# Attention and MLP backward pass on one core: the stores of the second to last pair move to GpSimd's queue in row pieces, and x is loaded in two pieces

## The chip, the core and the metric

The kernel runs on 1 core of a Trainium2 chip. The metric is the device time of one execution in microseconds (us). Sixteen DMA engines serve the core; a transfer is issued by one of the engine queues (SyncE, called SP; ScalarE, called ACT; GpSimd, called POOL), is cut into packets, and its packets are shared out over the DMA engines. Transfers issued by SP and ACT run on hardware rings, those issued by POOL on the software ring; in the profile these are the queues q1 (SP), q10 (ACT) and q0 (POOL). q8 and q14 carry instructions.

## What is computed

The forward function mixes a single-token attention block with a cache and a small MLP by a gate; the kernel returns its value and the gradients to nine inputs.

```python
q = (x @ wq).reshape(B, Sq, H, Dh)                  # Sq = 1, H = 32, Dh = 128, D = 640
scores = einsum("bhqd,bhkd->bhqk", q, k_cache) * Dh ** -0.5      # Sk = 4096
p = softmax(scores); o = einsum("bhqk,bhkd->bhqd", p, v_cache)
a = o.reshape(B, Sq, H * Dh) @ wo
h = B_x @ w1 + b1; b = (h * tanh(softplus(h))) @ w2              # F = 1728
g = sigmoid((x * gate_w).sum(-1))
out = g * a + (1 - g) * b                           # and the vjp with grad_out
```

Nearly all of the traffic is K and V, 32 MB each in bfloat16, which are read once, and dK and dV, of the same size, which are written once. dV of a head is the outer product of its softmax row and the gradient of its output, dK that of the score gradients and q.

## The kernel before

The 32 heads are worked in 16 pairs (`NP` = 16, numbered 0 to 15; `NP - 2` is pair 14). K or V of a pair is one tile `kv` of 128 partitions by 8192 bfloat16, 16 KB in each partition and 2 MB in all. Seven such buffers (`bufs`) are passed round: a load takes a buffer from `free_q`, VectorE writes the gradient over the loaded tile in place (`outer`, line 465, four quarters of 128x2048), the tile is stored, and the buffer goes back to `free_q`, where `pump` gives it to the next load. All loads of K and V are issued by SP. The order on every engine is written by hand: `slot(i, s)` lists what happens in each of 16 steps of pair i.

- Line 131 loads K or V; it waits until the store that frees the buffer has landed.
- `store_kv` (lines 734 to 738) issues the store of a pair's dV in step 13 of the pair and of its dK in step 3 of the next. While loads are left it is issued by POOL (25 stores); once the list of loads is empty it is issued by SP. Those are five: dK of pair 12, dV and dK of pair 13, dV and dK of pair 14.
- The last pair has no slots of its own after step 7. `last_dv(t)` and `last_dk(t)` make one quarter of dV or dK, and after quarters 1 and 3 SP stores the finished half (lines 875 and 881, 1 MB each).
- Between these quarters stand the sums and scalings for the gradients of `wq` (`dx_sum` on VectorE, `dwq_row` on ScalarE, stored by POOL, line 493) and of `wo` (`dwo_row` on ScalarE, stored by ACT, line 358), and behind them the final chain of small operations (lines 918 to 941) that ends in `frow`, three rows of 640 values which POOL stores (line 944).
- Lines 182 to 185 load x, gate_w, grad_out and b1 by POOL at the start; each is a tile of 128 partitions with a few values.

A store of 128 rows gives every DMA engine 8 rows of 16 KB: the 25 stores of POOL and the others of its kind show in the trace as 8 packets of 16,384 bytes on each of 16 engines.

Of the kernel before, what the change touches and what calls it, by code (L numbers as in the profile page):

```python
# [17 lines left out]
def kernel(  # L18
# [33 lines left out]
    nc = tc.nc  # L52
    P = 128
    _, H, Sk, Dh = A_k_cache.shape
# [3 lines left out]
    NP = H // 2  # L58
    NG = H // 8
    J = 64  # L60
# [26 lines left out]
    def vec_cols(v):  # L87
        return v.rearrange("(p c) -> p c", c=RC)

    x_v = A_x.rearrange("a b (p c) -> (a b p) c", c=RC)  # L90
    dy_v = grad_out.rearrange("a b (p c) -> (a b p) c", c=RC)
# [10 lines left out]
    def C(shape, dt, name):  # L102
        return const.tile(shape, dt, name=name, tag=name)
# [3 lines left out]
    bufs = [big.tile([P, bufw.get(i, KVW)], BF16, name=f"kv{i}", tag=f"kv{i}") for i in range(NBUF)]  # L107
# [4 lines left out]
    xc = C([P, RC], BF16, "xc")  # L112
    dyc = C([P, RC], BF16, "dyc")
    gwc = C([P, RC], BF16, "gwc")
# [7 lines left out]
    kbuf, vbuf, mbuf = {}, {}, {}  # L122
# [48 lines left out]
    def pump():  # L171
        while loads and (free_q or not loads[0][0]):
            loads.popleft()[1]()
# [5 lines left out]
        base=0, pattern=[[-1, P]], channel_multiplier=1,  # L179
    )  # L180
    pump()
    for t, src in ((xc[:], x_v), (gwc[:], vec_cols(gate_w)), (dyc[:], dy_v),
                   (b1c[:, 0:FK], B_b1[0:FM].rearrange("(p k) -> p k", k=FK)),
                   (b1c[0:FR, FK:FN], B_b1[FM:F].rearrange("(p o) -> p o", o=1))):
        nc.gpsimd.dma_start(t, src)
# [34 lines left out]
    def misc(shape, dt, name):  # L220
        return one_ps.tile(shape, dt, name=name, tag="misc")

    def chain(shape, dt, name):
        return one_ps.tile(shape, dt, name=name, tag="chain")
# [99 lines left out]
    def o_rows(g):  # L324
        ps = misc([P, 16, 8], F32, "o8_ps")
        nc.tensor.matmul(ps[:].rearrange("p a b -> p (a b)"), lhsT=od16[:].rearrange("p a b -> p (a b)"), rhs=idb[:],
                         start=True, stop=True)
        o8m = two.tile([P, 16, 8], F32, name="o8m", tag="o8m", bufs=1)
        nc.vector.tensor_tensor(o8m[:], ps[:], m16[:].unsqueeze(2).to_broadcast([P, 16, 8]), ALU.mult)
        nc.vector.reduce_sum(o8f[:], o8m[:].rearrange("p a b -> p b a"), axis=AX.X)  # L330
        nc.vector.tensor_copy(o8[:], o8f[:])

    def a_cols(g, c0=0, c1=RC):
        if c0 == 0:
            mst["a"] = misc([P, RC + W], F32, "a_ps")
        ps = mst["a"][:, 0:RC]
        wv = wob[g % 2][:].rearrange("p k (n c) -> p k c n", c=RC)
        for c in range(c0, c1):
            for k in range(8):
                nc.tensor.matmul(mst["a"][:, c:c + W], lhsT=wv[:, k, c, :], rhs=o8[:, k:k + 1].to_broadcast([P, W]),  # L340
                                 start=(k == 0), stop=(k == 7))
        if c1 == RC:
            if g == 0:
                nc.vector.tensor_copy(a_acc[:], ps)
            else:
                nc.vector.tensor_tensor(a_acc[:], a_acc[:], ps, ALU.add)

    def scaled(eng, dst, src, col):
        if eng is nc.vector:
            nc.vector.tensor_scalar(dst, src, col, None, ALU.mult)  # L350
        else:
            nc.scalar.mul(dst, src, col)  # L352
# [4 lines left out]
    def st_dwo(g, eng, k0=0, k1=8):  # L357
        eng.dma_start(dwo_v[g][:, k0:k1], wob[g % 2][:, k0:k1])
# [21 lines left out]
    def products(ps, src, c, col):  # L380
        for t in range(4):
            B = 4 * c + t
            for e in range(2):
                nc.tensor.matmul(ps[:, 4 * B:4 * B + W].rearrange("p (a b) -> p a b", b=4),  # L384
                                 lhsT=src[:, t, :, e],
                                 rhs=col[:, e, :, :].rearrange("p a b -> p (a b)").unsqueeze(1).to_broadcast([P, W // 4, 4]),
                                 start=(e == 0), stop=(e == 1))
# [74 lines left out]
    def outer(b, col, row, q):  # L462
        n = J // 4
        j0 = q * n
        nc.vector.tensor_tensor(  # L465
            kview(b)[:, j0:j0 + n, :].rearrange("p j (a b) -> p j a b", b=2),
            col[:, j0:j0 + n, :].unsqueeze(2).to_broadcast([P, n, Dh // 2, 2]),
            row.rearrange("p (a b) -> p a b", b=2).unsqueeze(1).to_broadcast([P, n, Dh // 2, 2]),
            ALU.mult)
# [5 lines left out]
    def dq_row(i):  # L475
        dqb = two.tile([P, 2], BF16, name="dqb", tag="dqb")
        nc.vector.tensor_copy(dqb[:], st[i]["dq"][:, 0:2])  # L477
        ps = chain([P, 2, P], BF16, "dqr_ps")
        for hh in range(2):
            nc.tensor.transpose(ps[:, hh, :], dqb[:, hh:hh + 1].to_broadcast([P, P]), idb[:])  # L480
        c = 256 * (i % 4)
        nc.scalar.copy(dqrow[(i // 4) % 2][:, c:c + 256].rearrange("p (a b) -> p a b", a=2), ps[:])
# [6 lines left out]
    def dwq_row(g, c0, c1, rc, eng=nc.scalar):  # L489
        scaled(eng, wqa[:, rc, g * GC + c0:g * GC + c1], dqrow[g % 2][:, c0:c1], xf[:, rc:rc + 1])  # L490

    def st_dwq(c0, c1, eng):
        eng.dma_start(dwq_v[:, :, c0:c1], wqa[:, :, c0:c1])
# [185 lines left out]
    for g in range(NG - 1):  # L679
        i = 4 * g + 4  # L680
# [16 lines left out]
    for g in (2, 3):  # L697
        i = 4 * g
# [8 lines left out]
    g, i = NG - 1, NP - 2  # L707
# [14 lines left out]
    def run_products(i, s):  # L722
# [5 lines left out]
        else:  # L728
# [2 lines left out]
                S_ps[n] = one_ps.tile([P, 2 * J + W], F32, name="S", tag="S")  # L731
            products(S_ps[n], src, s - 8, qR[(n // 4) % 2][:, n % 4])

    def store_kv(dct, i, dst, eng):
        b = dct[i]
        eng.dma_start(dst, bufs[b][:, 0:J * Dh])  # L736
        free_q.append(b)
        pump()

# [3 lines left out]
    def slot(i, s):  # L743
# [16 lines left out]
        if chain_on:  # L760
            if s == 0:
                dq_row(i - 1)
            if s in (0, 1, 3):
                dk_quarter(i - 1, (0, 1, 3).index(s) + 1)
            if s == 3:
                store_kv(kbuf, i - 1, dKv[i - 1], nc.gpsimd if loads else nc.sync)
            if s == 2:
                soft_max(i)
            if s == 4:
                soft_maxt(i)  # L770
            if s == 7:
                soft_z(i)
# [9 lines left out]
        if s in (9, 10, 12, 13):  # L782
            outer(vbuf[i], st[i]["p"], Dr[(i // 4) % 2][:, i % 4, :], (9, 10, 12, 13).index(s))
            if s == 13:
                store_kv(vbuf, i, dVv[i], nc.gpsimd if loads else nc.sync)
# [81 lines left out]
    i, g = NP - 1, NG - 1  # L867
# [3 lines left out]
    def last_dv(t):  # L871
        outer(vbuf[i], st[i]["p"], Dr[g % 2][:, q, :], t)
        if t % 2:
            h = slice((t - 1) * KVW // 4, (t + 1) * KVW // 4)
            nc.sync.dma_start(dVv[i][:, h], bufs[vbuf[i]][:, h])

    def last_dk(t):
        outer(fb, st[i]["ds"], Qr[g % 2][:, q, :], t)
        if t % 2:
            h = slice((t - 1) * KVW // 4, (t + 1) * KVW // 4)  # L880
            nc.sync.dma_start(dKv[i][:, h], bufs[fb][:, h])
# [12 lines left out]
    last_dv(0)  # L894
    for rc in range(RC):
        dwq_row(g, CA, CB, rc)
    o_rows(g)
    dq_row(i)
    last_dv(1)
    a_cols(g)  # L900
    for k in range(8):
        dwo_row(g, k)
        if k % 4 == 3:
            st_dwo(g, nc.scalar, k - 3, k + 1)
    last_dv(2)
    last_dv(3)
    last_dk(0)
    last_dk(1)
    for rc in range(RC):
        dx_sum(g, NG + g, CB, GC, rc)  # L910
        dwq_row(g, CB, GC, rc)
    st_dwq(g * GC + CA, (g + 1) * GC, nc.gpsimd)
    last_dk(2)
    last_dk(3)

    fin = C([P, 3, RC], BF16, "fin")
    ga = C([P, RC], F32, "ga")
# [8 lines left out]
                                   accum_out=dgp[:])  # L926
    dg_ps = chain([P, 1], F32, "dg_ps")
    nc.tensor.matmul(dg_ps[:], lhsT=ones_f[:], rhs=dgp[:], start=True, stop=True)
    dz = C([P, 1], F32, "dz")
    nc.vector.tensor_scalar(dz[:], dg_ps[:], g_all[:], omg[:], ALU.mult, ALU.mult)  # L930
    nc.vector.tensor_scalar(fin[:, 2, :], xf[:], dz[:], None, ALU.mult)
# [5 lines left out]
    fr_ps = misc([3, RC, P], BF16, "fr_ps")  # L937
    for c in range(RC):
        nc.tensor.transpose(fr_ps[:, c, :], fin[:, :, c], idb[:])
    frow = C([3, P, RC], BF16, "frow")  # L940
    nc.vector.tensor_copy(frow[:].rearrange("r p c -> r c p"), fr_ps[:])
    for r, v in enumerate((out_0.rearrange("a b n -> (a b) n"), out_1.rearrange("a b n -> (a b) n"),
# [31 lines left out]
```

## Time and profile before

| | us |
|---|---|
| three runs | 407.05, 407.87, 526.68 |
| median | 407.87 |
| the profiled execution, device time | 405.83 |
| its span, first to last instruction | 404.0 |

| engine | busy us | share of the span |
|---|---|---|
| TensorE matmul (PE) | 297.2 | 74% |
| VectorE (DVE) | 285.6 | 71% |
| ScalarE (ACT) | 246.8 | 61% |
| GpSimd (POOL) | 25.2 | 6% |

| DMA | |
|---|---|
| moved | 164.88 MB, mean 408 GB/s |
| read and written in HBM | 82.03 MB each |

The compute engines have idle time throughout; the DMA engines have hardly any before the last 12 us. The profile's lines name an engine, a line of the kernel, the operation, what is written and what is read. "SPq" and "POOLq" are the queues of SyncE and GpSimd, where DMAs are issued. The DMA share of a stretch of time is the mean over the 16 DMA engines, so that one engine alone is 1/16, or about 0.06.

### The profile page before, as it was taken

To read this page: it belongs to the slowest core of one execution; us is meant where nothing else is said; L and a number is where in the kernel's file an instruction comes from. 1 tells how busy PE (TensorE), PEld (TensorE's weight loads), DVE (VectorE), ACT (ScalarE), POOL (GpSimd) and SP (SyncE) were. 2 spreads that over 40 slices of the span, in tenths; PEclk is the share of its full clock that TensorE was granted. 3 is DMA by queue.
4 is the path that set the end of the run, shared out by engine and by line. 5 is a ranking of instruction groups with operands and counts; after the bars stand their busy time and mean duration, and the time that the engine had idled before them with its cause. 6 is when DMAs were issued, how large, how long until landed. Compare 5 with 4: busy or idle time off the path is not lost.

```text
span 404.0 us, 13041 instructions
## 1 busy us (share of the span) xinstructions
PE 297.2 (74%) x5654; PEld 272.9 (68%) x5657; DVE 285.6 (71%) x618; ACT 246.8 (61%) x507; POOL 25.2 (6%) x50
## 2 busy tenths in 40 slices
PE   4878996998885888673989869732989897987110
PEld 3558986877775777673889769732789786886100
DVE  2767695699975969583797839642695988597930
ACT  3555462586668678761766567731567996876800
POOL 3000100002000101000001000000000100000020
PEclk9999997998999899986999989985899998999555
DMA  8999999999999999999999999999999999999991
GB/s 275 426 399 434 420 423 417 430 418 420 423 422 427 391 421 429 427 431 430 428 423 428 426 427 426 425 426 432 431 406 400 414 428 419 422 430 422 420 386 44
DMA packets 15963, 164.88 MB, mean 408 GB/s; under 512 B 1713, under 2 KB 1905, under 8 KB 6178
## 3 DMA queue, kind: packets, MB, share of 16 engines
q1 hardware_dynamic: 8832, 94.08, 55.7%
q0 software_dynamic: 5472, 63.42, 37.3%
q10 hardware_dynamic: 1602, 6.56, 4.1%
q8 instruction: 44, 0.72, 0.7%
q14 instruction: 13, 0.11, 0.1%
HBM read 82.03 MB, written 82.03 MB: 406 GB/s over the span
## 4 chain that ended last, share of the span: by engine, by line
DMA 34%; issue 23%; PE 20%; DVE 12%; ACT 5%; POOL 2%; SPq 1%; POOLq 0%; ACTq 0%; DVEq 0%
DMA wq<-in_A_wq_dram 10%; DMA out_dram<-kv 8%; PE tr L374 8%; DVE kv L465 7%; DMA wq<-in_B_w_dram 6%; DMA wo<-in_A_wo_dram 5%; DMA kv<-in_A_k_cache_dram 5%; ACT tch L377 2%; PE dP L384 2%; PE o L433 2%; PE S L384 2%; PE dq L433 1%; PE q_ps L277 1%; PE a_ps L340 1%; DVE wq L486 1%
## 5 line engine op out<-in xcount | busy, mean ns | idle before, releaser
L374 PE MATMUL tr<-idf,kv 128*128 128x128 f32 x1024 | 172.1, 294 | 36.0 <-DMA kv<-in_A_v_cache_dram 20.0
L377 ACT COPY tch<-tr 128x512 f32<-128x512 f32 x256 | 144.2, 587 | 83.8 <-PE tr L374 78.6
L374 PEld LDWEIGHTS tr<-idf,kv 128*128 128x128 f32 x1024 | 118.6, 150 | 41.7 <-issue 36.9
L384 PEld LDWEIGHTS <-tch 128*128 128x128 bf16 x2048 | 89.5, 99 | 27.9 <-ACT tch L377 21.8
L465 DVE TENSOR_TENSOR kv<-p_dup,Dr 128x2048 bf16<-128x2048 bf16 x64 | 76.7, 1220 | 4.4 <-ACT p_dup L424 4.1
L465 DVE TENSOR_TENSOR kv<-ds_dup,Qr 128x2048 bf16<-128x2048 bf16 x64 | 76.8, 1220 | 0.4
L433 PEld LDWEIGHTS <-kv 128*128 128x128 bf16 x2048 | 59.1, 97 | 2.7 <-issue 1.6
L384 PE MATMUL dP<-dR,tch 128*128 128x48 bf16 x1024 | 47.3, 185 | 9.3 <-ACT tch L377 9.0
L384 PE MATMUL S<-qR,tch 128*128 128x48 bf16 x1024 | 48.1, 187 | 6.9 <-ACT tch L377 5.7
L290 DVE SCALAR_TENSOR_TENSOR junk<-wo,da_bc 128x640 bf16<-128x640 bf16 x32 | 26.3, 822 | 13.5 <-DMA wo<-in_A_wo_dram 12.7
L433 PE MATMUL o<-e_m,kv 128*128 128x48 bf16 x1024 | 32.4, 186 | 0.2 <-issue 0.2
L433 PE MATMUL dq<-ds_m,kv 128*128 128x48 bf16 x1024 | 30.6, 183 | 2.1 <-DVE ds_m L455 1.9
L736 POOL DMA_DIRECT2D out_dram<-kv x25 | 13.4, 537 | 296.0 <-DVE kv L465 278.6
L352 ACT ACTIVATE wq<-dqrow,xf 128x1024 bf16<-128x1024 bf16 (+2 forms) x30 | 25.1, 860 | 1.2 <-DVE wq L486 0.8
L486 DVE SCALAR_TENSOR_TENSOR wq<-wq,dqrow 128x1024 bf16<-128x1024 bf16 (+2 forms) x30 | 25.1, 863 | 0.2
L439 DVE TENSOR_TENSOR o<-o,rz 128x2 f32<-128x2 f32 x16 | 2.5, 158 | 26.5 <-PE o L433 26.5
L398 DVE TENSOR_REDUCE m<-S 64x1 f32<-64x64 f32 x32 | 7.0, 219 | 15.8 <-PE S L384 15.6
L424 ACT ACTIVATE p_dup<-e_m,rz 64x128 bf16<-64x128 bf16 x32 | 12.7, 397 | 7.8 <-DVE rz L418 7.4
L352 ACT ACTIVATE wo<-da_bc,o8f 128x640 bf16<-128x640 bf16 x20 | 15.9, 824 | 1.5 <-PE a_ps L340 0.9
L406 DVE TENSOR_REDUCE negM<-mt 64x1 f32<-64x64 f32 x32 | 7.1, 222 | 11.5 <-PE mt L403 10.8
L480 PE MATMUL dqr_ps<-idb,dqb 128*128 128x128 bf16 x32 | 4.9, 241 | 13.7 <-DVE dqb L477 13.7
L459 ACT COPY ds_dup<-ds_m 64x128 bf16<-64x128 bf16 x32 | 9.5, 297 | 8.1 <-DVE ds_m L455 7.6
(163 smaller groups left out, 253.2 us busy)
## 6 DMA issues: line engine op xcount, KB each, us to landing
out_dram<-kv POOLq DMA_DIRECT2D x25, 2048.0 KB, 19.8
kv<-in_A_v_cache_dram SPq DMA_DIRECT2D x16, 2048.0 KB, 19.8
kv<-in_A_k_cache_dram SPq DMA_DIRECT2D x15, 2048.0 KB, 20.6
out_dram<-kv SPq DMA_DIRECT2D x5, 2048.0 KB, 26.2
wo<-in_A_wo_dram SPq DMA_DIRECT2D x4, 1280.0 KB, 20.9
out_dram<-kv SPq DMA_DIRECT2D x4, 1024.0 KB, 20.5
out_dram<-wo POOLq DMA_DIRECT2D x3, 1280.0 KB, 26.8
wq<-in_A_wq_dram SPq DMA_DIRECT2D x2, 1280.0 KB, 9.5
```

What stands on the lines that cost most here:

```text
L290: nc.vector.scalar_tensor_tensor(junk[:], in0=wob[g % 2][:, k, :], scalar=1.0, in1=da_bc[:], op0=ALU.mult, op1=ALU.mult, accum_out=do8[g % ...
L352: nc.scalar.mul(dst, src, col)
L374: nc.tensor.transpose(tp[:, t, :], src[:, 4 * c + t, :], idf[:])
L377: nc.scalar.copy(dst[:].rearrange("p a b e -> p (a b e)").bitcast(F32), tp[:].rearrange("p a b -> p (a b)"))
L384: nc.tensor.matmul(ps[:, 4 * B:4 * B + W].rearrange("p (a b) -> p a b", b=4), lhsT=src[:, t, :, e], rhs=col[:, e, :, :].rearrange("p a b - ...
L406: nc.vector.tensor_reduce(negM[HS[hh]], mt[HS[hh], 64 * hh:64 * hh + 64], axis=AX.X, op=ALU.max, negate=True)
L424: nc.scalar.activation(p[HS[hh]], e_m[i % 2][HS[hh], :, hh].unsqueeze(2).to_broadcast([64, J, 2]), ACT.Copy, scale=st[i]["rz"][HS[hh], hh: ...
L433: nc.tensor.matmul(st[i][key][:].rearrange("p (a b) -> p a b", b=2), lhsT=src[:, j, :], rhs=rhs[:, j, :].unsqueeze(1).to_broadcast([P, W / ...
L459: nc.scalar.copy(ds[HS[hh]], ds_m[i % 2][HS[hh], :, hh].unsqueeze(2).to_broadcast([64, J, 2]))
L465: nc.vector.tensor_tensor(kview(b)[:, j0:j0 + n, :].rearrange("p j (a b) -> p j a b", b=2), col[:, j0:j0 + n, :].unsqueeze(2).to_broadcast ...
L486: nc.vector.scalar_tensor_tensor(w, in0=w, scalar=1.0, in1=dqrow[g % 2][:, c0:c1], op0=ALU.mult, op1=ALU.mult, accum_out=dq_acc[:, rc, par ...
L736: eng.dma_start(dst, bufs[b][:, 0:J * Dh])
```

## The change

Three things are edited. The store of dV of pair 14 becomes three transfers of 4, 120 and 4 rows and that of dK of pair 14 three of 13, 105 and 10 rows, all issued by POOL. The load of x becomes two transfers, of 60 and 68 rows. In the work of the last pair five of the quarters are moved: `last_dv(1)` ahead of `o_rows` and `dq_row`, `last_dv(2)` to where `last_dv(1)` was, `last_dk(1)` behind the `wq` sums, and `last_dk(2)` and `last_dk(3)` into the final chain, behind the two groups of matmuls in it.

```diff
-    for t, src in ((xc[:], x_v), (gwc[:], vec_cols(gate_w)), (dyc[:], dy_v),
+    for t, src in ((xc[0:60], x_v[0:60]), (xc[60:P], x_v[60:P]), (gwc[:], vec_cols(gate_w)), (dyc[:], dy_v),
...
+    late = {(True, NP - 2): (4, 120, 4), (False, NP - 2): (13, 105, 10)}
+
     def store_kv(dct, i, dst, eng):
         b = dct[i]
-        eng.dma_start(dst, bufs[b][:, 0:J * Dh])
+        p0 = 0
+        for n in late.get((dct is vbuf, i), (P,)):
+            (nc.gpsimd if n < P else eng).dma_start(dst[p0:p0 + n], bufs[b][p0:p0 + n, 0:J * Dh])
+            p0 += n
         free_q.append(b)
         pump()
...
     last_dv(0)
     for rc in range(RC):
         dwq_row(g, CA, CB, rc)
+    last_dv(1)
     o_rows(g)
     dq_row(i)
-    last_dv(1)
+    last_dv(2)
     a_cols(g)
     for k in range(8):
         dwo_row(g, k)
         if k % 4 == 3:
             st_dwo(g, nc.scalar, k - 3, k + 1)
-    last_dv(2)
     last_dv(3)
     last_dk(0)
-    last_dk(1)
     for rc in range(RC):
         dx_sum(g, NG + g, CB, GC, rc)
         dwq_row(g, CB, GC, rc)
     st_dwq(g * GC + CA, (g + 1) * GC, nc.gpsimd)
-    last_dk(2)
-    last_dk(3)
+    last_dk(1)
...
     nc.tensor.matmul(dg_ps[:], lhsT=ones_f[:], rhs=dgp[:], start=True, stop=True)
+    last_dk(2)
     dz = C([P, 1], F32, "dz")
...
         nc.tensor.transpose(fr_ps[:, c, :], fin[:, :, c], idb[:])
+    last_dk(3)
     frow = C([3, P, RC], BF16, "frow")
```

The bytes that are moved, and every compute instruction, are the same before and after; five DMA instructions are added (four on net for the stores, one for x), and two of SP's leave its queue for POOL's.

## The prediction

> **What bounds the kernel now.** I read the page first, its slices and its DMA queues.
>
> ```profile
> DMA  8999999999999999999999999999999999999991
> GB/s 275 426 399 434 420 423 417 430 418 420 423 422 427 391 421 429 427 431 430 428 423 428 426 427 426 425 426 432 431 406 400 414 428 419 422 430 422 420 386 44
> ...
> q1 hardware_dynamic: 8832, 94.08, 55.7%
> q0 software_dynamic: 5472, 63.42, 37.3%
> ```
>
> From the second slice to the second last the DMA engines are full, at about 425 GB/s, whatever the compute engines do. An edit to compute is therefore worth nothing unless it lets a DMA engine run dry. The queue lines give the price of a row: q0 moved 63.42 MB in 37.3% of 16 x 404.0 us, 2,411 us of engine time, so 16,384 bytes take 0.62 us on one DMA engine; q1 (94.08 MB, 55.7%) gives 0.63. The two rings cost the same per byte.
>
> The last slice is empty, so I then read the busy time of the last stretches.
>
> ```profile
> 390.00:392.00 2.00, 0.00 (x0) 0.00 (x0) 0.00 (x0) 0.00 (x0) 0.81 (x2) 0.50 0.99 407
> 392.00:394.00 2.00, 0.00 (x0) 0.00 (x0) 0.00 (x0) 0.00 (x0) 0.00 (x0) 0.50 0.59 243
> 394.00:396.00 2.00, 0.00 (x0) 0.00 (x0) 0.00 (x0) 0.00 (x0) 0.00 (x0) 0.50 0.29 118
> 396.00:398.00 2.00, 0.00 (x0) 0.00 (x0) 0.00 (x0) 0.00 (x0) 0.00 (x0) 0.50 0.07 29
> 398.00:400.00 2.00, 0.00 (x0) 0.00 (x0) 0.00 (x0) 0.00 (x0) 0.00 (x0) 0.50 0.06 25
> 400.00:402.00 2.00, 0.00 (x0) 0.00 (x0) 0.00 (x0) 0.00 (x0) 0.00 (x0) 0.50 0.07 29
> 402.00:404.00 2.00, 0.00 (x0) 0.00 (x0) 0.00 (x0) 0.00 (x0) 0.00 (x0) 0.50 0.00 0
> ```
>
> The last two columns are the DMA share and GB/s. From 392 to 396 the engines fall out one by one; from 396 to 402 the share is 0.06 to 0.07, which is 1/16: one DMA engine works alone for 6 us. In the packet records its last packets are 8192-byte packets of q1, end to end, the last done at 402.2; the other fifteen end between 391.7 and 396.1, at 394.1 in the mean. The waits of SP's queue say the same.
>
> ```profile
> SPq L969 <- DMA out_dram<-wq: 11.2, 1, 11.2
> SPq L969 <- DMA out_dram<-kv: 7.3, 1, 7.3
> ```
>
> After its last issue SP waits 11.2 us for the store of `wq`, then 7.3 us more for the last half of dK. The chain of waits ends in `frow` and shows none of this, so it isn't used. The lateness is old: of the last load of V fifteen shares landed between 355.7 and 360.1 and the sixteenth at 365.7. The records carry no engine number.
>
> **The change, part by part.** *Row pieces.* Both whole stores give each DMA engine 8 rows, so 16 together. If the piece of 120 is 8 rows on each of fifteen engines and that of 105 is 7 on each, and the same engine is left out of both, it keeps only its share of the small pieces: 0 to 4 rows, 12 to 16 fewer, or 7.5 to 10 us at 0.625. The 4 + 4 + 13 + 10 = 31 single rows go mostly to the others, which then have 15 + 2 = 17 rows against 16, +0.6 us (+1.2 for an engine with 18). No transfer of before shows an uneven split of wide rows, so I bound it: at best the late engine ends at 402.2 - 7.5 = 394.7 or sooner; at worst it is not the one left out and ends at 402.8. In the first case the other fifteen set the end, 396.1 + 0.6 = 396.7, a gain of 5.5 us. I take this one: a piece of 120 or 105 rows has a whole split over 15 and none over 16, so one engine is spared, and the edit names the same one for both.
>
> [...]
>
> *Issue.* POOL's stores take 0.53 us each, SP's 0.33. Six issues put 3.2 us on POOL, in order ahead of the `wq` store at 361.4, which moves to about 366. POOL waited 19.6 us before that store and 21.7 before the next; nobody reads these tiles again. SP loses two issues. Cost 0; if POOL were full, up to 3.2 us. POOL's issues also wait for the landing of its eighth issue before; for the last `frow` rows those are now the dV pieces of about 359, which have 28 us to land against a median of 26.2 for such stores on SP. Cost 0 to 1, off the path.
>
> *Order of rings.* 4 MB move from q1 to q0 at 358 and 365. V of pair 15 has mostly landed by 360, and no later load exists, so no compute waits longer. With both rings full an engine alternates; the total per engine is unchanged. Cost 0.
>
> *Quarters moved.*
>
> ```profile
> 377.33 2.36 DVE L465 TENSOR_TENSOR kv<-ds_dup,Qr 128x2048 bf16<-128x2048 bf16 x2
> ...
> 381.33 2.36 DVE L465 TENSOR_TENSOR kv<-ds_dup,Qr 128x2048 bf16<-128x2048 bf16 x2
> ...
> 387.07 1.91 DVE L941 COPY frow<-fr_ps 3x640 bf16<-3x640 bf16 x1 [0.79 <-PE fr_ps L939]
> 389.27 1.53 POOL L944 DMA_DIRECT2D out_dram<-frow  x3 [4.51 <-DVE frow L941]
> ```
>
> A quarter is 1.14 us (2.27 for two). dV's first half goes out some 1.5 us sooner (before at 374.2), dK's first half about 1 later (1.73 us of `wq` sums come ahead of its second quarter, less 0.8 gained above). Its second half waits also for the final chain: from dk1's end near 380.7, 0.85 of small operations, 1.14, 1.1, 1.14: issued near 385.0 instead of 383.7. `frow` fills its two waits for PE with these quarters and leaves near 387.2 instead of 389.3. At 385 the engines still have about 9 us of work, of which that half is 1 MB / 425 GB/s = 2.5 us, so 6.5 us lie ahead of it: cost 0. If an engine ran dry there, it would cost the 1.3 us of delay.
>
> *x.* One more POOL issue, 0.54 us, ahead of gate_w. VectorE waits 1.33 us for gate_w at 8.58, so the first stage starts about 0.5 us later. The prefetched loads and the stores of 41.3 and 47.2 keep the DMA engines full past 60 us, so the cover holds: 0, else 0.5.
>
> **Sum.** 402.2 to 396.7 is -5.5 us; all else 0 to +1.3. On the profiled execution, 405.83 - 5.5 = 400.3 (span 398.5). The two close runs are 1.2 and 2.0 us above that execution; the mean of the three is 406.9, so I expect 401.4 in unprofiled runs. Against the median of 407.87 that is -1.6%.
>
> **Rivals.**
> - *The late engine isn't the spared one.* Nothing in the records says which it is. It then gets up to one row more: 405.83 + 0.6 = 406.4, or 407.5 from the mean. For it: any of sixteen engines could be meant. Against it: the lateness is steady, 5 to 9 us in each of SP's transfers from 340 on, so it is one engine, which a fixed choice of rows can hit. [...]
> - *Slower: the pieces fall on few engines.* If 120 rows went to 8 engines and 105 to 7 (15 each), an engine in both would have 30 rows and some 2 single ones instead of 16: 16 x 0.625 = +10 us, so that the late one ends at 412.2, device time 415.8, 416.9 from the mean; on one engine the 105 rows alone are 65 us. It decides from 15 rows more on the late engine (9.1 us, from the mean to 2% above the median). For it: the only odd transfer of before, one row on ACT, has one data packet. Against: the 64-row transfers of `w2` land with their 128-row neighbours (25.4 and 25.8 us).
> - *Deeper gain.* If the single rows fall on the early ones of the fifteen and the order evens the rest, the end is their mean, 394.1, plus 0.6: a gain of 7.5, 399.4 from the mean, and a little over half of such cases below the 2% line.
>
> **Chances.** Forecast 0.60, at 401.4, its own range 398.8 to 404. Spared the wrong engine 0.18, near 407.5. Few engines 0.08, 416 and up. Deeper gain 0.14. A measurement of this kernel tells about 2%, 8.2 us, from no change, so faster means below 399.7. Faster: 0.08 of the deeper case and 0.10 of the forecast's low side = 0.18. Slower: 0.08. Same: 0.74. The range takes in the forecast, nearly all of the deeper gain, and the wrong engine: 398.3 to 408.3.
>
> **What would show it.** The lone engine's 6 us at the end must be gone: a DMA share that falls from 1.0 to 0 within some 5 us, with the last kv landing near 397 and SP's last wait for kv near 1 to 2 us instead of 7.3. The wrong engine shows as the same six microseconds at 0.06; few engines as a long stretch at 0.06 to 0.5 after 396. The second dK half should be issued near 385 and `frow` near 387, with a DMA share of 1.0 until 392; a dip there would break the claim that the moved quarters cost nothing. A GB/s below 415 between 360 and 385 would show that pieces cost more than whole stores, which I priced at nothing.

## The result, and the profile after

The changed kernel takes 416.86 us (median of 4 runs, 415.8 to 417.18) against 407.46 us for the kernel before (median of 4), a ratio of 1.0239, 95% interval 1.0201 to 1.0276: slower by 9.4 us (one run of the kernel before, the 526.68 us of the table, is far off and not in the ratio). The forecast was 401.4 and the range ended at 408.3, so the time is outside it. The profiled execution took 415.8 us, with a span of 414.0.

The page of the changed kernel, the slices and the two large DMA queues:

```profile
DMA  8999999999999999999999999999999999999980
GB/s 269 424 401 419 427 419 427 424 416 380 427 428 416 394 422 429 429 430 426 427 429 424 430 426 426 426 427 428 429 417 421 423 423 413 427 346 274 333 336 39
...
q1 hardware_dynamic: 8544, 89.89, 52.7%
q0 software_dynamic: 5904, 67.61, 40.0%
```

The DMA row reads 9 from the second slice to the third last, much as before: the engines count as busy. The row under it tells another story. A slice is 10.35 us here, and in slices 36 to 39, from 362 to 404 us, the engines move 346, 274, 333 and 336 GB/s; the same four slices of the kernel before had 430, 422, 420 and 386. From 370 to 380 us the share is 0.96 at 274 GB/s against 1.01 at 425 before: the share hides a loss of rate that the bytes show. The stretches of the end, of the changed kernel and then three of the kernel before (the last two columns are DMA share and GB/s, the one ahead of them the granted TensorE clock):

```profile
360.00:370.00 10.00, 8.14 (x175) 7.70 (x174) 8.60 (x24) 8.03 (x18) 3.98 (x7) 1.00 1.01 380
370.00:380.00 10.00, 3.57 (x92) 3.07 (x88) 3.93 (x10) 2.70 (x7) 0.00 (x0) 0.71 0.96 274
380.00:390.00 10.00, 2.58 (x44) 2.39 (x44) 8.91 (x26) 7.03 (x11) 0.00 (x0) 0.50 0.95 303
390.00:400.00 10.00, 0.69 (x5) 0.41 (x5) 3.80 (x7) 1.42 (x4) 2.36 (x4) 0.50 1.00 386
400.00:404.00 4.00, 0.00 (x0) 0.00 (x0) 0.00 (x0) 0.00 (x0) 0.00 (x0) 0.50 0.56 229
404.00:406.00 2.00, 0.00 (x0) 0.00 (x0) 0.00 (x0) 0.00 (x0) 0.00 (x0) 0.50 0.19 77
406.00:408.00 2.00, 0.00 (x0) 0.00 (x0) 0.00 (x0) 0.00 (x0) 0.00 (x0) 0.50 0.14 57
408.00:410.00 2.00, 0.00 (x0) 0.00 (x0) 0.00 (x0) 0.00 (x0) 0.00 (x0) 0.50 0.09 35
410.00:412.00 2.00, 0.00 (x0) 0.00 (x0) 0.00 (x0) 0.00 (x0) 0.00 (x0) 0.50 0.04 16
```

```profile
360.00:370.00 10.00, 7.88 (x171) 7.38 (x171) 7.77 (x27) 6.89 (x17) 0.84 (x1) 1.00 1.00 420
370.00:380.00 10.00, 3.70 (x107) 3.46 (x107) 8.54 (x16) 7.74 (x15) 0.00 (x0) 0.77 1.01 425
380.00:390.00 10.00, 1.25 (x7) 0.91 (x7) 7.28 (x24) 3.23 (x7) 1.55 (x3) 0.50 1.01 423
```

Two things are to be seen. The rate falls in the stretch in which POOL issues the first three pieces, at 360.09; and the thin tail, a share of 0.19 to 0.04 from some late engines and at last a single one, is still there, from 404 to 411. The kernel before moved 420, 425 and 423 GB/s in the three stretches from 360 to 390, so 0.40 + 1.51 + 1.20 = 3.1 MB were not moved there, which take 7.3 us at 425 GB/s, of the 10.0 us by which the span grew.

The two waits of SP's queue after its last issue:

```profile
SPq L974 <- DMA out_dram<-frow: 18.4, 2, 17.4
...
SPq L974 <- DMA out_dram<-kv: 0.5, 1, 0.5
```

The wait for `kv` has shrunk from 7.3 to 0.5, as the forecast asked. It proves nothing: SP now waits up to 17.4 us for the store of `frow` first, and the `kv` lands 0.5 us after that. How a long wait is shared out between two names says only which transfer the late engine finishes last: the last shares of `frow` and of the last `kv` land at 411.14 and 411.73.

The records of single packets give the size of it. All packets of 16 KB on the two rings between 362 and 390 us, mean and longest, in ns:

| kernel | mean | longest |
|---|---|---|
| before | 616 | 1006 |
| after | 831 | 2844 |
| before 360 us, both | 619 to 621 | |

### The profile page after: what moved, and what is told of

Same layout as the page of the kernel before. It is cut to its first block, busy times and chain, and to the rows that moved or that the text cites. A ratio compares the mean times of both kernels' runs of the same rounds, so it can differ in the third digit from the quotient of the medians.

```text
span 414.0 us, 13053 instructions
## 1 busy us (share of the span) xinstructions
PE 299.8 (72%) x5657; PEld 276.3 (67%) x5657; DVE 285.0 (69%) x618; ACT 247.2 (60%) x507; POOL 28.8 (7%) x57
## 4 chain that ended last, share of the span: by engine, by line
DMA 34%; issue 24%; PE 21%; DVE 10%; ACT 4%; POOL 2%; SPq 1%; DVEq 0%; POOLq 0%; ACTq 0%
DMA wq<-in_A_wq_dram 9%; PE tr L374 8%; DMA out_dram<-kv 7%; DMA kv<-in_A_k_cache_dram 6%; DMA wq<-in_B_w_dram 6%; DVE kv L465 6%; DMA wo<-in_A_wo_dram 5%; PE o L433 2%; PE dq L433 2%; PE dP L384 2%; ACT tch L377 2%; PE S L384 2%; PE q_ps L277 1%; PE a_ps L340 1%; POOL out_dram L740 1%
## 5 line engine op out<-in xcount | busy, mean ns | idle before, releaser
L433 PEld LDWEIGHTS <-kv 128*128 128x128 bf16 x2048 | 60.1, 98 | 8.7 <-issue 7.6
L740 POOL DMA_DIRECT2D out_dram<-kv x31 | 16.5, 533 | 314.8 <-DVE kv L465 292.4
L433 PE MATMUL dq<-ds_m,kv 128*128 128x48 bf16 x1024 | 31.5, 184 | 7.7 <-issue 5.3
L482 ACT COPY dqrow<-dqr_ps 128x256 bf16<-128x256 bf16 x16 | 6.1, 379 | 14.8 <-PE dqr_ps L480 14.8
```

The lines of the kernel that those rows point to most:

```text
L433: nc.tensor.matmul(st[i][key][:].rearrange("p (a b) -> p a b", b=2), lhsT=src[:, j, :], rhs=rhs[:, j, :].unsqueeze(1).to_broadcast([P, W / ...
L740: (nc.gpsimd if n < P else eng).dma_start(dst[p0:p0 + n], bufs[b][p0:p0 + n, 0:J * Dh])
```

## The experiments

The experiments of one group ran on one chip and share their runs of the kernel before.

### First group: which part, and is it the ring or the row pieces

Theory one after the result: a store of fewer than 128 rows runs at a lower rate than a whole one, whatever ring it is on. Rivals: the software ring is slower here, or delays the loads of V; or the moved quarters let the engines run dry.

**e1_whole_on_pool**: all of the change, but each of the two stores is one transfer of 128 rows, issued by POOL.

```diff
-    late = {(True, NP - 2): (4, 120, 4), (False, NP - 2): (13, 105, 10)}
+    late = {(True, NP - 2): (P,), (False, NP - 2): (P,)}
...
-            (nc.gpsimd if n < P else eng).dma_start(...)
+            (nc.gpsimd if (dct is vbuf, i) in late else eng).dma_start(...)
```

> The changed kernel with the two stores of pair 14 whole, 128 rows each, but still on POOL's ring; x in two pieces and the quarters moved as in the change. Theory A (the row pieces themselves slow the DMA packets: 16 KB packets take 0.61 us before 360 us and 0.86 to 0.99 us on average between 365 and 390 in the changed kernel): all packets back at 0.61 us, GB/s of 360 to 390 back above 410, ratio to before 0.995 to 1.005. Theory B (two more whole stores on the software ring late in the kernel cost the time, cut or not): ratio 1.015 to 1.025, packets slow as in the change. Theory C (the moved quarters and x starve the DMA engines): ratio 1.02.

Measured: 406.34 us (10 runs) against 406.21 (19), ratio 1.0014 (1.0002 to 1.0026). Its stretches:

```profile
360.00:370.00 10.00, 8.23 (x190) 7.81 (x186) 8.31 (x23) 8.03 (x18) 1.59 (x3) 1.00 1.01 424
370.00:380.00 10.00, 4.30 (x116) 3.83 (x112) 8.46 (x19) 6.06 (x12) 0.00 (x0) 0.78 1.00 422
380.00:390.00 10.00, 1.25 (x7) 0.91 (x7) 8.04 (x23) 5.09 (x9) 2.33 (x4) 0.50 1.01 424
```

The rate is whole again. So the ring, together with x and the quarters, costs 0.3% at most, and the loss hangs on the cut into rows.

**e2_pieces_alone**: the kernel before with the row pieces only (x whole, quarters where they were).

```diff
+    late = {(True, NP - 2): (4, 120, 4), (False, NP - 2): (13, 105, 10)}
```

> The kernel before with the row pieces (4, 120, 4; 13, 105, 10) on POOL alone; x whole, no quarter moved. Theory A: ratio 1.02 to 1.03, slow packets between 360 and 395 us. Theory C: ratio 0.985 to 1.00. [...]

Measured: 414.63 us (4 runs), ratio 1.0204 (1.0185 to 1.0223): 8.4 us of the 9.4.

```profile
360.00:370.00 10.00, 7.88 (x171) 7.38 (x171) 7.77 (x27) 6.85 (x18) 2.46 (x4) 1.00 1.03 368
370.00:380.00 10.00, 4.57 (x107) 4.16 (x107) 4.13 (x10) 3.79 (x10) 0.00 (x0) 0.65 0.93 274
380.00:390.00 10.00, 0.56 (x2) 0.50 (x2) 9.15 (x24) 7.23 (x12) 0.84 (x1) 0.50 0.98 326
```

The same low rates as in the changed kernel, without the other two edits.

**e3_x_and_quarters**: the change without the row pieces; both stores stay whole on SP's ring.

```diff
-    late = {(True, NP - 2): (4, 120, 4), (False, NP - 2): (13, 105, 10)}
+    late = {}
```

> The changed kernel with the stores of pair 14 left whole on SP as before: x in two pieces and moved quarters alone. Theory A and B: ratio 0.995 to 1.005, one DMA engine alone for some 6 us at the end as before. Theory C: ratio 1.02.

Measured: 407.05 us (10 runs), ratio 1.0026 (1.0011 to 1.0040). The two other edits cost something, about 1 us, and are no part of the large loss.

**e4_halves_64**: the kernel before with both stores cut evenly, 64 + 64 rows on POOL. Sixty-four rows divide evenly over sixteen engines, 4 rows each, so that no engine need be spared; in e5 such stores reach 16 packets of 16 KB under way. From e1 it differs in the number of rows of a transfer, and in that x and the quarters are as before.

```diff
+    late = {(True, NP - 2): (64, 64), (False, NP - 2): (64, 64)}
```

> The kernel before with both stores of pair 14 in two pieces of 64 rows on POOL. Each piece splits evenly, 4 rows on each of 16 engines, so no engine gets more than before. [...] Theory A2 (what costs is the uneven split over 15 or fewer engines): packets at 0.61 us, ratio 0.995 to 1.005.

Measured: 410.07 us (4 runs), ratio 1.0121 (1.0071 to 1.0172).

```profile
360.00:370.00 10.00, 8.13 (x185) 7.71 (x181) 8.31 (x24) 8.01 (x18) 2.62 (x5) 1.00 1.02 360
370.00:380.00 10.00, 5.09 (x115) 4.48 (x110) 5.38 (x14) 4.38 (x10) 0.00 (x0) 0.70 1.01 283
380.00:390.00 10.00, 0.56 (x2) 0.50 (x2) 9.12 (x26) 6.76 (x12) 0.83 (x1) 0.50 0.97 326
...
404.00:406.00 2.00, 0.00 (x0) 0.00 (x0) 0.00 (x0) 0.00 (x0) 0.00 (x0) 0.50 0.13 53
406.00:408.00 2.00, 0.00 (x0) 0.00 (x0) 0.00 (x0) 0.00 (x0) 0.00 (x0) 0.50 0.02 8
```

An even cut loses the rate as well: the missing bytes, 0.60 + 1.42 + 0.97 = 3.0 MB, are as many as with the uneven pieces. So it is not the uneven split. Yet the kernel is only 3.9 us late by the medians (4.9 by the ratio; one of its four runs took 414.16, as long as e2), and the tail of one engine is nearly gone (0.13 and 0.02 instead of six microseconds at 0.06 and more). Why the late engine catches up here and not in the changed kernel was not settled.

### The disputed cost by itself

**e5_stores_alone**: computes nothing of the reference. It loads one tile of V and stores it into the places of dV and dK in different ways, each way after the one before has landed (a write to the first column of the tile stands between); every other output stays unwritten. Where a way's last store does not read that column, the next way starts beside it: so the end of the column halves overlaps with the start of the HBM block, and the end of that with the four neighbouring rows on POOL, which are therefore read from SP's ring alone.

```diff
+    phase(g, whole, 2)
+    phase(g, pieces(64, 64), 2)
+    phase(g, pieces(4, 120, 4), 2)
+    phase(g, pieces(13, 105, 10), 2)
+    phase(g, cols, 2)         # 128 rows, two halves of the columns
+    phase(g, block, 2)        # half the columns of 128 rows into 64 whole rows of HBM
+    phase(g, four(0, 1), 1)   # 4 neighbouring rows; then every 4th, every 32nd
...
+    phase(s, whole, 2)        # the same on SP's ring
+    phase(s, pieces(64, 64), 2)
+    phase(s, pieces(4, 120, 4), 2)
```

> A kernel that computes nothing of the reference: one 2 MB tile of V is loaded, and then stored in one way after another, each way alone on the chip (the next waits until the last has landed), 4 MB each unless said otherwise. On POOL's ring: whole; 64 + 64 rows; 4 + 120 + 4; 13 + 105 + 10; 128 rows in two halves of the columns; 128 rows by half of the columns written to the 1 MB of HBM that 64 rows fill; then single stores of 4 rows of 16 KB taken from neighbouring partitions, from every fourth, and from every 32nd partition. Then on SP's ring: whole; 64 + 64; 4 + 120 + 4; the three of 4 rows. [...] Theory A2 (the uneven split costs): 64 + 64 as fast as whole. Theory A3 (the rows of a piece collide in HBM): the half-column stores into the 64-row region are as slow as 64 + 64. Theory B2 (a matter of the software ring): slow on POOL, fast on SP.

Its stretches, one for each way; a row has busy time of VectorE and POOL, the granted clock, DMA share and GB/s. In order: whole, 64 + 64, 4 + 120 + 4, 13 + 105 + 10, column halves and the HBM block on POOL; whole, 64 + 64 and 4 + 120 + 4 on SP.

```profile
10.00:20.00 10.00, 0.00 (x0) 0.00 (x0) 1.00 0.97 408
22.00:40.00 18.00, 0.00 (x0) 0.96 (x2) 1.00 0.92 226
42.50:61.50 19.00, 0.00 (x0) 1.67 (x4) 1.00 0.73 218
64.00:82.00 18.00, 0.00 (x0) 1.89 (x4) 1.00 0.75 225
85.00:93.00 8.00, 0.00 (x0) 0.65 (x2) 1.00 1.01 409
94.00:102.00 8.00, 0.00 (x0) 1.46 (x3) 1.00 0.98 400
115.50:125.00 9.50, 0.00 (x0) 0.00 (x0) 1.00 0.98 414
127.00:145.00 18.00, 0.00 (x0) 0.00 (x0) 1.00 0.90 219
147.00:165.00 18.00, 0.00 (x0) 0.00 (x0) 1.00 0.77 230
```

Whatever takes all 128 rows of the tile moves 400 GB/s or more in its stretch, also with half the columns (409) and into a block of 64 rows of HBM (400). The cuts by rows move little more than half of that, 218 to 230, on either ring, with a DMA share of 0.92 for the even halves. So the rate hangs on which rows of the tile a store takes at one time, and not on the ring or on the place in HBM. At no time are more than 15 packets of 16 KB under way in the ways with 120 and 105 rows, where the whole and the 64 + 64 stores reach 16: the middle pieces leave out one engine, as the change meant them to. The packet records, from the first packet of a way to its last, give it more exactly:

| way | GB/s | packet of 16 KB |
|---|---|---|
| whole, either ring | 419 | 0.62 us (mean) |
| 64 + 64, POOL / SP | 228 / 225 | 1.22 / 1.25 (median) |
| 4 + 120 + 4, POOL / SP | 215 / 220 | 0.89 (mean), up to 3.98 |
| 13 + 105 + 10, POOL | 224 | 0.92 (mean), up to 3.66 |
| 4 neighbouring rows (SP) | 26 | 2.16 to 2.34 |
| 4 rows, every 4th | 98 | 0.61 |
| 4 rows, every 32nd | 51 | 1.14 to 1.24 |

The last three ways store four rows each and differ in nothing but which rows these are; GB/s times the time of a packet gives, as an estimate, 3.4 to 3.9 packets under way in the mean for each of the three. Neighbours take nearly four times as long as rows that stand 4 apart (2.16 to 2.34 us a packet against 0.61), rows 32 apart twice as long (1.14 to 1.24). Why is not shown: the records give the time of a packet, not what it waits for. The 215 GB/s of 4 + 120 + 4 on POOL is a mean too: 257 from 43 to 53 us and 170 from 53 to 61.

What these rates make of the change, as an estimate with nothing else running beside them: the two stores, 2.10 MB each, take 2.10 / 215 + 2.10 / 224 = 9.75 + 9.36 = 19.1 us against 10.0 at 419, so 9.1 us more. In the kernel, where other transfers run beside the pieces, e2 measured 8.4. The changed kernel is 416.86 - 406.34 = 10.5 us above e1, which differs from it in the cut alone, though in other groups of runs.

### Which engine is late, and which is spared

The packet records name no engine. A small load of m rows stands in SP's ring behind what is queued there, and a size of its own tells its packets from others. It is taken to put one packet on each of the first m engines, counted from 0; no record shows that by itself, and every index below rests on it. Where a late packet lands then tells which sets of engines the late one is in. The marks read a few columns of K into an unused part of a buffer.

**e6_marks_before**: the kernel before with marks of 1, 4, 6, 7, 8, 11 and 15 rows behind SP's last store.

```diff
+    def mark(m, n):
+        ...
+        nc.sync.dma_start(bufs[W1B][0:m, KVW + c:KVW + c + n], Kv[0][0:m, c:c + n])
...
+    for m in (1, 4, 6, 7, 8, 11, 15):
+        mark(m, 20 + m)
```

> The kernel before with seven tiny loads behind the last store of dK in SP's ring, of 1, 4, 6, 7, 8, 11 and 15 rows, each of another size, into unused columns of a buffer. Their packets are the last on each DMA engine. If a load of m rows runs on the first m engines, one row on each, then the engine that works alone at the end tells its number by which of them it carries. [...] Time about 1.00 to 1.01 of before.

Measured: 406.98 us against 406.16, one run each. The engine that is last carried the marks of 6, 7, 8, 11 and 15 rows, which landed on it at 402.85 to 402.91, and not those of 1 and 4. If m rows go to the first m engines, it is the fifth or sixth, index 4 or 5. Index 6 and higher are excluded by the mark of 6 rows.

**e7_marks_after**: the changed kernel with marks of 6, 7 and 15 rows right after the store of dK of pair 13 in SP's ring, and of 1, 6, 7, 8 and 15 at the end.

```diff
+    for m in (6, 7, 15):
+        mark(m, 40 + m)
...
+    for m in (1, 6, 7, 8, 15):
+        mark(m, 20 + m)
```

> The changed kernel with the same kind of marks behind the store of dK of pair 13 (6, 7 and 15 rows) and behind the last store (1, 6, 7, 8, 15 rows). The engine that has no row of 120 and 105 has next to nothing in POOL's ring and reaches the first marks 10 us or more before the others. [...] If pieces always start at the first engine: it carries none of them (the last engine). If the late engine at the end is the spared one, its tail is gone; else 3 to 7 us of one engine alone remain, carrying the same marks as in the kernel before.

Measured: 414.94 us. The engine that is alone at the end, from 408.9 to 411.07, carries the marks of 6, 7, 8 and 15 rows and not that of 1: by the same reading index 1 to 5, which takes in the late engine of e6. At the earlier marks that of 15 rows is first reached at 368.47, that of 6 at 371.01 and that of 7 at 372.24: no engine that carries 6 or 7 rows stands out as early. So by that reading the spared engine is none of those with index 0 to 6.

**e8_marks_fine**: the same places with marks of 5, 15 and 16 rows.

```diff
+    for m in (5, 15, 16):
+        mark(m, 40 + m)
...
+    for m in (5, 15, 16):
+        mark(m, 20 + m)
```

> The changed kernel with marks of 5, 15 and 16 rows behind dK of pair 13 and behind the last store. In the kernel before the late engine carried the marks of 6 rows and more and not those of 1 and 4, so it is the fifth or the sixth engine; in the changed kernel engine 6, counted from 0, was not early at the marks. Theory E (a piece starts at the first engine and the ring takes as many rows a share as fill 16 engines, so 120 and 105 rows spare the last engine): the engine that carries the marks of 16 rows but not those of 15 reaches them first, several us before any other. Theory F (the spared engine lies elsewhere): that engine is in the middle. The mark of 5 rows on the late engine tells 4 from 5.

Measured: 415.67 us. The last engine carries the mark of 5 rows, at 411.84; with e6 it is by that reading index 4, the fifth, given that it is one engine in both kernels and on the two chips that ran them. At the earlier marks one engine is first by more than 4 us, at 366.1 against 370.46, and it carries the mark of 16 rows but none of 15: by the same reading the pieces spare the last engine, index 15. The lead is less than the 10 us that e7 expected. POOL issues dK's pieces only at 365.73, so engine 15 stands out by dV's pieces; that 105 rows leave out the same engine as 120 is inferred.

### The two small edits by themselves

**e9_x_alone**: the kernel before with x in two pieces.

```diff
-    for t, src in ((xc[:], x_v), (gwc[:], vec_cols(gate_w)), ...
+    for t, src in ((xc[0:60], x_v[0:60]), (xc[60:P], x_v[60:P]), (gwc[:], vec_cols(gate_w)), ...
```

> The kernel before with x loaded in two pieces and nothing else. The prediction priced it at 0, at most 0.5 us: ratio 0.999 to 1.001.

Measured: 407.28 us (12 runs) against 406.50 (23), ratio 1.0022 (1.0007 to 1.0037), 0.9 us. VectorE's first steps with x and gate_w, from the timeline of e9 and then of the kernel before (start, length, what ended the wait):

```profile
9.21 0.17 DVE L799 CAST xf<-xc 128x5 f32<-128x5 bf16 x1 [5.80 <-DMA xc<-in_A_x_dram]
9.58 0.17 DVE L801 CAST gwf<-gwc 128x5 f32<-128x5 bf16 x1 [0.20 <-DMA gwc<-in_gate_w_dram]
...
10.84 0.15 DVE L811 TENSOR_SCALAR den<-en 128x1 f32<-128x1 f32 x1 [0.88 <-ACT en L809]
```

```profile
7.08 0.17 DVE L799 CAST xf<-xc 128x5 f32<-128x5 bf16 x1 [3.67 <-DMA xc<-in_A_x_dram]
8.58 0.17 DVE L801 CAST gwf<-gwc 128x5 f32<-128x5 bf16 x1 [1.33 <-DMA gwc<-in_gate_w_dram]
...
10.40 0.15 DVE L811 TENSOR_SCALAR den<-en 128x1 f32<-128x1 f32 x1 [1.44 <-ACT en L809]
```

In this pair x itself comes 2.13 us later, gate_w 1.00, and the first stage is 0.44 late at `den`. The other profiles agree on x alone: VectorE reads it at 7.08 to 7.67 in the five kernels that load it whole and at 8.39 to 9.21 in the six that cut it, but `den` starts at 9.98 to 10.53 and at 10.12 to 10.84. A late first stage is therefore not shown, and what costs the 0.9 us stays open.

**e10_quarters_alone**: the kernel before with the five quarters moved.

```diff
+    last_dv(1)
     o_rows(g)
     dq_row(i)
-    last_dv(1)
+    last_dv(2)
...
-    last_dk(2)
-    last_dk(3)
+    last_dk(1)
...
+    last_dk(2)
...
+    last_dk(3)
```

> The kernel before with the quarters of the last pair moved and nothing else. The prediction priced it at 0, 1.3 us if a DMA engine ran dry. Together with x it cost 0.26% (1 us). If the quarters carry that: ratio 1.001 to 1.004, and the late engine's end moves with the later issue of the last half of dK or with its backlog; if not, 0.999 to 1.001 and x carries it.

Measured: 406.64 us (12 runs), ratio 1.0002 (0.9987 to 1.0016). No cost of the quarters is to be seen, which leaves the load of x (0.22% alone) for the 0.26% of e3; e1, which has both edits, is 0.14% above the kernel before.

## Why the prediction was wrong, point by point

- **The bound.** DMA engines full from the second slice on, and edits to compute worth nothing: right. e10 moves five quarters of VectorE and changes nothing. One reading beside it was wrong: the landings from 355.7 to 365.7 are those of SP's first store, issued at 340.40; the last load of V, issued at 340.02, landed from 349.5 to 352.8 and its sixteenth share at 358.3. The lateness is the same, so nothing in the sum hangs on it.
- **The rings cost the same per byte.** Right for whole stores: e1 moves 4 MB to the other ring at 1.0014. The order of the rings, priced at 0, cost nothing either.
- **The price of a row in a piece: the step that failed.** The forecast took 0.625 us for each row of the pieces, the price of whole stores, and gave "A GB/s below 415 between 360 and 385" as the sign that this was wrong. The rate there was 380 and 274. The pieces move 215 to 224 GB/s instead of 419, with 0.89 to 0.92 us for a packet of 16 KB in the mean instead of 0.62 (e5). The price was 8 to 9 us (e2, e5) where the sum had zero, and it is what puts the time outside the range; that the -5.5 did not come either is the next point. All stores that the trace of before had of this kind were whole, so the price was not in it; the forecast priced it by the nearest row and kept no other end. The 64-row transfer for `w2` that landed with its neighbours (25.4 and 25.8 us, stores of its gradient by POOL), which it named against few engines, was no test of the price either: it is 80 KB, and how long it was queued hides how long its packets took.
- **The spared engine is the late one.** Also wrong. By the marks the late engine is index 4 (e6, e8) and the spared one index 15 (e8), and the tail stayed, at 404 to 411. That the pieces leave out one engine is shown (never more than 15 packets of 16 KB under way in e5); that it is the late one, on which the -5.5 us rests, was the author's estimate, and no run shows it. The two loads of x are of rows that 16 does not divide either: in the trace of the changed kernel the 60 rows went out with fifteen packets of four rows (40 bytes) and the 68 with thirteen of five rows (50 bytes) and a rest. This was the first rival; its condition came true, its +0.6 us did not, because the price of the pieces lay on top. Had the late engine been the spared one, the 5.5 us of the forecast would, by these numbers, still be less than the 9 us that the cut costs.
- **The slower rival.** Its 416.9 us is the time measured, by another way. No engine got 30 rows: the middle pieces used 15 engines each (15 packets under way for most of the time in e5). The nearness of the numbers confirms nothing.
- **Issue.** Six issues by POOL were to cost 3.2 us in order; the timeline of the changed kernel shows 1.56 and 1.55.

```profile
360.09 1.56 POOL L740 DMA_DIRECT2D out_dram<-kv  x3 [14.74 <-DVE kv L465]
366.53 1.55 POOL L740 DMA_DIRECT2D out_dram<-kv  x3 [4.88 <-DVE negM L406]
368.06 0.89 POOL L493 DMA_DIRECT2D out_dram<-wq  x1
```

  The `wq` store moved to 368.06, near the 366 of the forecast, and POOL had waited ahead of both groups: cost 0, as said.
- **Quarters.** Cost 0, right (e10). The second half of dK was to be issued near 385 and `frow` near 387; in e1, which has the quarters moved and whole stores, the pair of dK issues takes 4.37 us from 382.38, which puts the second near 386.4, and `frow` leaves at 388.51. Both are some 1.4 us later than forecast, inside the cover of 6.5 us.
- **x.** Priced at 0, "else 0.5". Measured 0.9 us (e9, interval 0.3 to 1.5), of the order of the other end; but the late first stage that was to cause it is not borne out by the other profiles, so whether the cover failed stays open.
- **Work of the compute engines after 370.** Not in the forecast: in the changed kernel they run late as well, VectorE busy 3.93 us between 370 and 380 against 8.46 in e1, and the pair of dK issues begins at 388.08 against 382.38. TensorE stands at `dq`, with nothing in the profile that it waits for (the changed kernel, then e1):

```profile
372.03 0.92 PE L433 MATMUL dq<-ds_m,kv 128*128 128x48 bf16 x30 [0.98 <-DVE ds_m L455]
377.99 1.54 PE L433 MATMUL dq<-ds_m,kv 128*128 128x48 bf16 x34 [5.04 <-issue]
```

```profile
371.58 1.78 PE L433 MATMUL dq<-ds_m,kv 128*128 128x48 bf16 x64 [0.98 <-DVE ds_m L455]
```

  The packet records point at late instructions. q8, which carries instructions, has a packet of 16 KB every 6 to 9 us from 346 to 375 in the kernel before; in the changed kernel one comes 13 us after the last, at 375.59 to 376.53, and TensorE goes on 1.46 us after its end. In e1 that packet came at 369.26, and `dq` ran through. In the other four kernels with cut stores (e2, e4, e7, e8) TensorE stops after the same 30 matmuls and goes on 1.2 to 1.4 us after the end of that packet. That it is late because slowed packets stand ahead of it on its engine fits and was not shown. The stop can have cost the DMA engines little: their share is 0.96, 0.95 and 1.00 between 370 and 400, so they lacked work for 0.9 us of the 30 at most.

Open: why the engine of index 4 is late, and whether sparing it would bring the tail's 6 us. It is behind rather than slow: the last 20 packets of 8 KB of the kernel before, nearly all its own, take 0.309 us each, as those of all engines between 375 and 392 do. And it falls behind in the course of the kernel: where a transfer of 128 rows lands before 170 us, its last share comes at most 1.6 us after the one before it; until 240 us that is at most 2.2, until 290 at most 5.6, and after that up to 9.7. In the whole stores of e5 it is at most 0.1 us. A transfer that leaves out this engine and keeps the rate of a whole store, 419 GB/s, was not found, so that was not tried, and no version here is faster than the kernel before.

## What to carry to other kernels

Do not cut a large store by partitions to even out the DMA engines: alone, a transfer that takes all 128 rows moved at 419 GB/s here and halves of 64 rows at 228; if it must be cut, cut the columns (409 in its stretch). Read the GB/s beside the DMA share, since the share can be near 1.0 while each packet takes longer (0.92 at 226 GB/s and 1.22 us a packet in e5, where whole stores have 0.97 at 408 and 0.62). Before work is taken off one engine, find out which it is: marks of a few rows on the ring did that here in three runs.

## What the runs showed of the hardware that was not expected

- The rate of a store hangs on which rows it takes at one time: 4 neighbouring rows 26 GB/s, 4 rows that stand 4 apart 98 (e5).
- A load of 10 bytes for each of 128 partitions, cut in two, brings x 0.7 to 2.1 us later (all profiles) and costs 0.9 us of 407 (e9), by a way that was not found.
- Even halves of 64 rows lose as many bytes between 360 and 390 as the uneven pieces of e2, 3.0 MB each, but end 4.6 us sooner than those (e4 410.07 against e2 414.63), with hardly a tail of one engine.
